# A gated mix of linear attention and a mixture of experts: sums by head as fp32 products in four column strips, reciprocals spread through scratch memory

## The chip, the cores and the metric

The kernel runs on one core of a Trainium2 chip. TensorE (PE) multiplies matrices: it holds a weight tile of up to 128 x 128 (loaded by a row named PEld) and streams up to 512 columns through it, into PSUM. VectorE (DVE), ScalarE (ACT) and GpSimd (POOL) work on up to 128 partitions by some hundred elements. DMA transfers are issued by the sequencer of SyncE (SP), of GpSimd or of ScalarE, each in its own order. The metric is the device time of one execution in microseconds (us), lower is better.

## The reference

Sequence 2048, width 512, 32 heads of 16, 8 experts of 1792 hidden units, all experts used for each token (K = E = 8), everything in fp32:

```python
phi = lambda t: jnp.where(t > 0, t + 1, jnp.exp(t)) + 1e-6
pq, pk = phi(q), phi(k)
kv = jnp.einsum("bhsd,bhse->bhde", pk, v)
z = jnp.einsum("bhsd->bhd", pk)
num = jnp.einsum("bhqd,bhde->bhqe", pq, kv)
den = jnp.einsum("bhqd,bhd->bhq", pq, z)[..., None] + 1e-6
o = num / den
...
a = o @ wo
b = sum over e of softmax(x @ w_gate)[e] * (silu(x @ w1[e]) @ w2[e])
g = sigmoid((x * gate_w).sum(-1, keepdims=True))
out = g * a + (1 - g) * b
```

(The last lines are condensed.) The change concerns `den`: for each query and head a sum over the head's 16 features of phi(q) times z, its reciprocal times the gate g, and the product of that with phi(q).

## The kernel before, in words

**Number format.** Most products run in a reduced fp32 type (F32R). To keep precision, each operand is split into a high part (a rounded copy) and a low part (the remainder), and `mm3` (lines 57 to 60) issues three products: high by high, high by low, low by high. Its lines 58, 59 and 60 in the profile are most of TensorE's work. Plain fp32 products exist in few places: the state (L885), the folding of the output weights (`fold`, L895, four products with 512 moving columns) and the normaliser (L904).

**Stages.** `keys` projects the keys and collects sums over the sequence. `experts` then runs one long loop over ticks `u`. In a tick, `up` issues the products of the first expert layer (group `g = u // 7`, step `k = u % 7`) and `tick(n)`, with `n = u - 58`, those of the second layer, each time as one level of a seven-product block scheme. A tick is filled with six products of each, twelve in all; `other()` is the work of VectorE, ScalarE and the queues beside them, issued ahead of the tick's second-layer products, and `mid()` issues these and what is to follow them. The order is written out by hand; each engine works through its own instructions in that order. The attention output is treated as one more expert (parts `A`), whose "hidden" values are phi(q) times the reciprocals.

**Queries.** phi(q) is computed early and put into DRAM scratch (`pqd`, one 128 x 512 tile for each of 2 x 2 blocks of 512 queries and 4 chunks of features). Beside four of the expert parts (`m.beside`) the loop works on one block `i` of 512 queries each. `s` counts the ticks from the part's start:

- `s = -3`, `queries_load` (L953 on): on SP's queue the sums z (`zcd`, high and low parts, 2 x 32 columns for each chunk) and a spreading matrix of zeros and ones (`spd`) come into one raw tile `Q.az`, and the four chunks of phi(q) into another.
- `s = 0..3`, `queries_first`: ScalarE makes the high part of phi(q) + EPS (L63, tile `az`), VectorE the low part (L86). `queries_last` (L996): TensorE multiplies both by `Q.z[:, s]`, 64 weight columns (32 heads by the high z, 32 by the low z), into one bank `dn` with the tag "a", accumulating over the four chunks.
- `s = 4`: ScalarE copies the low half out of PSUM, VectorE adds the high half (L976): `Q.r`, 32 heads x 512 queries.
- `s = 5..8`: VectorE takes reciprocals, 128 columns a tick (L980). `s = 9`: it multiplies by the gate (L982). `s = 10`: high part by ScalarE, remainder by VectorE (L985), into rows of `Q.un`.
- `s = 14..17`: TensorE multiplies the spreading matrix with these (L1000), so that each of the 128 features of a chunk has its head's reciprocal, in a PSUM bank with the tag "a".
- `s = 15..18`: VectorE multiplies phi(q) + EPS by it (L988), and SP stores the chunk back to `pqd`.

Accumulations into `acct` (L815) go by GpSimd's queue, two or so at the end of a part's phases; between `s = 5` and `s = 18` of a block there is none. `normaliser` (L901 to L911) computes z once, early in the loop. Tiles with the tag "a" share two PSUM banks; "rm" (raw tiles) has two buffers, "ot" (`out_tile`) four.

Of the kernel before, what the change touches and what calls it, by code (L numbers as in the profile page):

```python
# [37 lines left out]
def f32(ap):  # L38
    return ap.bitcast(F32)


@with_exitstack
def gated_mix_kernel(ctx: ExitStack, tc: tile.TileContext, xT, x, wk, wv, wqkv_q, wo, wm, out):
    nc = tc.nc
    PS = bass.MemoryType.PSUM

    const = ctx.enter_context(tc.tile_pool(name="const", bufs=1))
    xpool = ctx.enter_context(tc.tile_pool(name="xpool", bufs=14))
    w1p = ctx.enter_context(tc.tile_pool(name="w1p", bufs=1))
    psum = ctx.enter_context(tc.tile_pool(name="psum", bufs=1, space=PS))  # L50
    dram = ctx.enter_context(tc.tile_pool(name="dram", bufs=1, space=bass.MemoryType.DRAM))
    ctx.enter_context(tc.manual_schedule())

    m = SimpleNamespace(nc=nc, tc=tc, const=const, xpool=xpool, w1p=w1p, psum=psum, v=nc.vector,
                        xT=xT, x=x, wk=wk, wv=wv, wq=wqkv_q, wo=wo, wm=wm, out=out)

    def mm3(ps, wh, wlo, xh, xl, start, stop):
        nc.tensor.matmul(ps, wh, xh, start=start, stop=False, skip_group_check=True)  # L58
        nc.tensor.matmul(ps, wh, xl, start=False, stop=False, skip_group_check=True)  # L59
        nc.tensor.matmul(ps, wlo, xh, start=False, stop=stop, skip_group_check=True)  # L60

    def act_copy(dst, src, scale=1.0, bias=0.0):
        nc.scalar.activation(dst, src, AF.Copy, scale=scale, bias=bias)  # L63

    def ps_tile(name, tag, bufs=None):
        return psum.tile([P, TB], F32, name=name, tag=tag, bufs=bufs or {"a": 2, "b": 1, "c": 1, "dn": 4}[tag])

    m.mm3, m.act_copy, m.ps_tile = mm3, act_copy, ps_tile


    def phi_first(dst, src):
        nc.scalar.activation(dst, src, AF.Exp)
        nc.scalar.activation(src, src, AF.Relu)

    def phi_last(dst, src):
        nc.vector.scalar_tensor_tensor(dst, dst, 1.0, src, op0=ALU.min, op1=ALU.add)

    def phi(dst, src):
        phi_first(dst, src)
        phi_last(dst, src)  # L80

    def eps_high(h, d):
        act_copy(h, d, bias=EPS)

    def eps_low(lo, d, h):
        nc.vector.scalar_tensor_tensor(lo, d, EPS, f32(h), op0=ALU.add, op1=ALU.subtract)  # L86

    m.phi, m.phi_first, m.phi_last, m.eps_high, m.eps_low = phi, phi_first, phi_last, eps_high, eps_low
    m.ident = const.tile([P, P], F32, name="ident")


    def x_tile(name, tag="x"):
        return xpool.tile([P, 2, TB], F32R, name=name, tag=tag, bufs=14 if tag == "x" else 2)

    m.x_tile = x_tile
    m.XO = [[None] * 7, [None] * 7]
    m.xstash = dram.tile([7, 2, P, 2 * TB], F32, name="xstash")
    m.w2stash = [dram.tile([P, 2, D], F32, name=f"w2stash{i}") for i in range(7 * (E * NPAIR + 2) // 2)]
    m.wgtd = dram.tile([E + 1, S], F32, name="wgtd")
    m.acct = dram.tile([2, 2, KT, P, TB], F32, name="acct")  # L100
    m.pqd = dram.tile([2, 2, KT, P, TB], F32, name="pqd")
    m.wpd = [dram.tile([P, D], F32, name=f"wpd{c}") for c in range(KT)]
    m.zcd = dram.tile([P, KT * 2 * NH], F32, name="zcd")
    m.spd = dram.tile([P, KT * P], F32, name="spd")

    X = [[SimpleNamespace(e=e, h=h, n=NPAIR) for e in range(E)] for h in range(2)]
    A = m.A = [SimpleNamespace(e=E, h=h, n=2) for h in range(2)]
    M = E // 2  # L110

    m.parts = [*X[0], *X[1][:M], A[0], *X[1][M:], A[1]]
    at = 0
    for part in m.parts:
        part.t0, at = at, at + 7 * part.n
    m.NTICK = at
    m.groups = [(part, q) for part in (A[0], *X[0], *X[1][:M], A[1], *X[1][M:]) for q in range(part.n)]
    m.NG = len(m.groups)
    for part in m.parts:
        part.gs = [g for g, (p, _) in enumerate(m.groups) if p is part]  # L120
    m.G1 = X[1][0].gs[0]

    m.beside = [*X[1][:2], *X[1][M:M + 2]]

    misc = ExitStack()
    m.misc = misc.enter_context(tc.tile_pool(name="misc", bufs=1, side="right"))


    def pad(pool):
        nc.gpsimd.memset(pool.tile([P, 24], F32, name="pad", tag="pad", bufs=1), 0.0)  # L130

    m.pad = pad
    weights(m)
    keys(m)
    experts(m, misc)


# [181 lines left out]
def keys(m):  # L319
# [113 lines left out]
    def bands(t):  # L433
        if t == 5:
            band(mask.rearrange("p (b e) -> p b e", e=DH), [[-DH, P // DH], [0, DH]], 1)
        elif t == 6:
            band(maskh, [[P, KT], [-DH, NH]], 1)
        elif t == 7:

            spread = m.w1p.tile([P, 2, D], F32, name="spread", tag="ws", bufs=2)[:, 0]  # L440
            nc.gpsimd.memset(spread[2 * NH:], 0.0)
            for i in range(2):
                band(spread[i * NH:(i + 1) * NH].rearrange("p (c f) -> p c f", c=KT), [[P, KT], [1, P]], -DH)
            nc.gpsimd.dma_start(m.spd, spread)

    pk = {}

# [130 lines left out]
def experts(m, misc):  # L578
# [322 lines left out]
    def normaliser():  # L901
        ps = ps_tile("z", "dn")[:, :KT * NH]
        for c in range(KT):
            nc.tensor.matmul(ps[:, c * NH:(c + 1) * NH], m.pks[:, c * P:(c + 1) * P], m.ones, start=(c == 0),  # L904
                             stop=True, skip_group_check=True)
        zf = r_tile("zf")[:, :KT * NH].rearrange("p (c f) -> p c f", c=KT)
        zc = r_tile("zc", F32R)[:, :2 * KT * NH].rearrange("p (c j f) -> p c j f", c=KT, j=2)
        v.scalar_tensor_tensor(zf, ps.rearrange("p (c f) -> p c f", c=KT), S * EPS, m.maskh, op0=ALU.add, op1=ALU.mult)
        v.tensor_copy(zc[:, :, 0], zf)
        v.tensor_sub(zc[:, :, 1], zf, f32(zc[:, :, 0]))  # L910
        nc.sync.dma_start(m.zcd, f32(zc).rearrange("p c j f -> p (c j f)"))  # L911

    def gates(step):
        g = m.lg[:, :, :E]
# [33 lines left out]

    Q = SimpleNamespace()

    def queries_load(i):  # L953
        if i % 2 == 0:
            Q.az = m.raw_tile(f"az{i}", F32R)
            Q.z = Q.az[:, :2 * KT * NH].rearrange("p (c f) -> p c f", c=KT)
            Q.spread = Q.az[:, 2 * KT * NH:2 * KT * NH + D].rearrange("p (c f) -> p c f", c=KT)
            Q.un = Q.az[:, 2 * KT * NH + D:2 * KT * NH + 3 * D].rearrange("p (j t) -> p j t", j=2)
            nc.sync.dma_start(f32(Q.az[:, :2 * KT * NH]), m.zcd)
            nc.sync.dma_start(f32(Q.az[:, 2 * KT * NH:2 * KT * NH + D]), m.spd)  # L960
        Q.d = m.raw_tile(f"pq{i}").rearrange("p (c t) -> p c t", c=KT)
        for c in range(KT):
            nc.sync.dma_start(Q.d[:, c], m.pqd[i // 2, i % 2, c])

    def queries_first(i, s):
        h, j = divmod(i, 2)
        if 0 <= s < KT:
            m.eps_high(Q.un[:, 0], Q.d[:, s])
            m.eps_low(Q.un[:, 1], Q.d[:, s], Q.un[:, 0])
        elif s == 4:  # L970
            r = Q.r = out_tile(f"r{i}")[:NH]
            Q.gate = out_tile(f"rg{i}")[:NH]
            at = (2 * h + j) * TB
            nc.sync.dma_start(Q.gate, m.wgtd[E:E + 1, at:at + TB].to_broadcast([NH, TB]))
            act_copy(r, Q.ps[NH:2 * NH], bias=EPS)
            v.tensor_add(r, Q.ps[:NH], r)  # L976
            nc.gpsimd.memset(f32(Q.un[2 * NH:, 0]), 0.0)
        if 5 <= s < 9:
            r = Q.r[:, (s - 5) * P:(s - 4) * P]
            v.reciprocal(r, r)  # L980
        elif s == 9:
            v.tensor_mul(Q.r, Q.r, Q.gate)  # L982
        elif s == 10:
            act_copy(Q.un[:NH, 0], Q.r)
            v.tensor_sub(Q.un[NH:2 * NH, 0], Q.r, f32(Q.un[:NH, 0]))  # L985
        if 15 <= s < 15 + KT:
            d = Q.d[:, s - 15]
            v.scalar_tensor_tensor(d, d, EPS, Q.ps, op0=ALU.add, op1=ALU.mult)  # L988
            nc.sync.dma_start(m.pqd[h, j, s - 15], d)

    def queries_last(i, s):
        if 0 <= s < KT:
            if s == 0:
                Q.ps = ps_tile(f"dn{i}", "a")
            for j in range(2):
                nc.tensor.matmul(Q.ps[:2 * NH, :], Q.z[:, s], Q.un[:, j], start=(s == 0 and j == 0),  # L996
                                 stop=(s == KT - 1 and j == 1))
        elif 14 <= s < 14 + KT:
            Q.ps = ps_tile(f"n{i}_{s}", "a")
            nc.tensor.matmul(Q.ps, Q.spread[:, s - 14], Q.un[:, 0], start=True, stop=True)  # L1000


    def load_query(part, i):
# [227 lines left out]
```

## Time and profile before

| | |
|---|---|
| three runs | 2349.44, 2350.26 (median), 2350.53 us |
| the profiled execution | 2350.77 us, its span 2349.1 us |
| mean granted TensorE clock | 0.999 |
| VectorE, share of the span | 77% |
| ScalarE, share of the span | 60% |
| GpSimd, share of the span | 7% |

Rows of the profile read: line, engine, operation, tile written <- tiles read, shape, count; then busy time in us and the mean duration in ns. In the view by tile, a row has the shortest, median and longest duration in ns and the first and last start. In the timeline, a row has its start and its duration in us. A TensorE row begins when the product is issued and its end is modelled, so rows of following products overlap.

### The profile page before, as it was taken

How to read it: one execution, taken by the hardware profiler on the slowest of the kernel's cores; microseconds unless marked ns; L12 is line 12 of the kernel's file. 1: busy time of each engine (PE TensorE's matmuls, PEld its weight loads, DVE VectorE, ACT ScalarE, POOL GpSimd, SP SyncE). 2: the span in 40 equal slices, each digit the busy share in tenths (PEclk: the TensorE clock that was granted, in tenths of full speed). 3: DMA queues.
4: the chain of work that ended last, by engine and by line, in shares of the span. 5: the costliest groups of instructions: out<-in, count | busy, mean ns of one | idle time of the engine just before them, and what ended most of it. 6: DMA issues, size and time to landing. Idle time of an engine off the chain costs nothing.

```text
span 2349.1 us, 31301 instructions
## 1 busy us (share of the span) xinstructions
PE 2338.4 (100%) x10492; PEld 1935.4 (82%) x10492; DVE 1811.9 (77%) x3102; ACT 1419.3 (60%) x2655; POOL 158.7 (7%) x222
## 2 busy tenths in 40 slices
PE   9999999999999999999999999999999999999999
PEld 8877888888888888888888888888888888888887
DVE  6798888888888888888677768776676777766666
ACT  6686666666666656666555555555565655555553
POOL 2101000000000000000000000000011000000101
PEclk9999999999999999999999999999999999999999
DMA  7898888988889898988845455654556655555566
GB/s 225 239 311 249 264 288 249 278 263 267 268 267 275 256 290 252 271 269 262 287 144 170 152 172 153 182 186 144 163 166 188 182 150 174 162 166 166 165 220 207
DMA packets 299345, 513.23 MB, mean 218 GB/s; under 512 B 24352, under 2 KB 193840, under 8 KB 298800
## 3 DMA queue, kind: packets, MB, share of 16 engines
q1 hardware_dynamic: 274992, 464.10, 59.8%
q0 software_dynamic: 23344, 46.49, 10.8%
q8 instruction: 82, 1.34, 0.2%
q10 hardware_dynamic: 848, 0.66, 0.1%
q14 instruction: 79, 0.65, 0.1%
HBM read 343.43 MB, written 163.52 MB: 216 GB/s over the span
## 4 chain that ended last, share of the span: by engine, by line
PE 97%; DVE 1%; DMA 1%; issue 0%; ACT 0%; POOL 0%; DVEq 0%; ACTq 0%; POOLq 0%
PE p L58 16%; PE p L60 16%; PE p L59 16%; PE a L58 8%; PE a L60 8%; PE a L59 8%; PE c L59 4%; PE c L58 4%; PE c L60 4%; PE b L60 2%; PE b L59 2%; PE b L58 2%; PE g L451 2%; DMA w2stash<-w 1%; PE y L58 1%; PE y L60 1%
## 5 line engine op out<-in xcount | busy, mean ns | idle before, releaser
L58 PE MATMUL p<-ho,w 128*128 128x512 f32 x1620 | 631.4, 390 | 0.8 <-DVE d L844 0.6
L60 PE MATMUL p<-ho,w 128*128 128x512 f32 x1620 | 630.3, 389 | 0.0
L59 PE MATMUL p<-ho,w 128*128 128x512 f32 x1620 | 630.3, 389 | 0.0
L760 DVE TENSOR_TENSOR ho<-s,ho 128x512 fp32r<-128x512 f32 x784 | 537.2, 686 | 71.2 <-ACT ho L63 67.6
L63 ACT ACTIVATE ho<-s 128x512 fp32r<-128x512 f32 x784 | 487.3, 623 | 21.0 <-PE p L60 8.5
L58 PEld LDWEIGHTS p<-ho,w 128*128 128x128 f32 x1620 | 304.0, 188 | 66.7 <-ACT p L63 1.8
L60 PEld LDWEIGHTS p<-ho,w 128*128 128x128 f32 x1620 | 304.2, 188 | 63.2
L59 PEld LDWEIGHTS p<-ho,w 128*128 128x128 f32 x1620 | 304.1, 188 | 63.0
L63 ACT ACTIVATE o<-rs 128x512 fp32r<-128x512 f32 x224 | 129.1, 576 | 172.7 <-PE a L60 111.7
L690 DVE TENSOR_TENSOR s<-c,s 128x512 f32<-128x512 f32 x116 | 80.2, 692 | 188.6 <-PE c L60 178.7
L63 ACT ACTIVATE o<-rm 128x512 fp32r<-128x512 f32 x240 | 137.5, 573 | 99.8 <-PE a L60 77.4
L63 ACT ACTIVATE s<-a 128x512 f32<-128x512 f32 x116 | 69.5, 599 | 146.9 <-PE a L60 140.3
L63 ACT ACTIVATE ws<-rm 128x512 fp32r<-128x512 f32 x203 | 114.7, 573 | 66.2 <-DMA w2stash<-ws 59.3
L619 ACT ACTIVATE s<-s 128x512 f32<-128x512 f32 x224 | 138.7, 619 | 9.9 <-DVE s L696 6.6
L619 ACT ACTIVATE s<-b 128x512 f32<-128x512 f32 x112 | 67.2, 600 | 112.4 <-PE b L60 100.3
L205 DVE TENSOR_TENSOR o<-rm,o 128x512 fp32r<-128x512 f32 x180 | 122.9, 683 | 0.1
L205 DVE TENSOR_TENSOR o<-rs,o 128x512 fp32r<-128x512 f32 x168 | 114.5, 681 | 0.6 <-ACT o L63 0.6
L219 DVE TENSOR_TENSOR ws<-rm,ws 128x512 fp32r<-128x512 f32 x154 | 105.5, 685 | 0.5 <-ACT ws L63 0.5
L696 DVE TENSOR_TENSOR s<-a,s 128x512 f32<-128x512 f32 x116 | 80.0, 689 | 32.8 <-PE a L60 32.5
L63 ACT ACTIVATE b<-a 128x512 f32<-128x512 f32 x116 | 67.1, 579 | 58.1 <-PE a L60 58.0
L63 ACT ACTIVATE s<-c 128x512 f32<-128x512 f32 x116 | 69.0, 595 | 25.6 <-PE c L60 25.6
L815 POOL DMA_DIRECT2D acct<-c x30 | 25.6, 854 | 794.8 <-DVE c L809 779.8
(321 smaller groups left out, 4540.5 us busy)
## 6 DMA issues: line engine op xcount, KB each, us to landing
w<-w2stash SPq DMA_DIRECT2D x403, 512.0 KB, 4.0
w2stash<-ws SPq DMA_DIRECT2D x357, 256.0 KB, 4.2
rm<-wm SPq DMA_DIRECT2D x228, 256.0 KB, 5.2
rs<-wm SPq DMA_DIRECT2D x108, 256.0 KB, 4.0
wb<-wgtd SPq DMA_DIRECT2D x16, 512.0 KB, 5.2
acct<-c POOLq DMA_DIRECT2D x30, 256.0 KB, 5.6
acct<-d POOLq DMA_DIRECT2D x30, 256.0 KB, 5.5
acct<-k POOLq DMA_DIRECT2D x30, 256.0 KB, 5.5
```

Of the source, the lines that this page charges most:

```text
L58: nc.tensor.matmul(ps, wh, xh, start=start, stop=False, skip_group_check=True)
L59: nc.tensor.matmul(ps, wh, xl, start=False, stop=False, skip_group_check=True)
L60: nc.tensor.matmul(ps, wlo, xh, start=False, stop=stop, skip_group_check=True)
L63: nc.scalar.activation(dst, src, AF.Copy, scale=scale, bias=bias)
L205: v.tensor_sub(two(o, 1), src, f32(two(o, 0)))
L219: v.tensor_sub(two(w, 1), src, f32(two(w, 0)))
L451: nc.tensor.matmul(ps, xk((0, 0, 1)[j], tb, k, tt * P, (tt + 1) * P), gw[g][:, (0, 1, 0)[j], k, :], start=(k == 0 and j == 0), stop=(k == ...
L619: nc.scalar.activation(dst, src, AF.Silu)
L690: v.tensor_add(sn[g, 2], bank[g, "c"], sn[g, 2])
L696: v.tensor_add(sn[g, 3], bank[g, "a"], sn[g, 3])
L760: v.tensor_sub(h[1], s, f32(h[0]))
L815: nc.gpsimd.dma_start(m.acct[part.h, j, dt], s, accum_op=ALU.add)
```

## The change

The sums by head are taken with plain fp32 products, without splitting. z is kept as one fp32 matrix, 32 columns a chunk. Chunk c's product goes to partitions 32c to 32c + 31 of one bank, so the four products have four different column strips of the array and do not accumulate onto each other: z is masked by head (`maskh`), so of the 32 heads in each strip only the chunk's own eight have a sum. All four are issued in tick 3. EPS is added to phi(q) in place by ScalarE. The copy out of PSUM, the reciprocals and the gate's product run on all 128 partitions. The spreading matrix and its products are gone: the eight rows of each strip that hold sums are written to a DRAM scratch `rd`, and read back with each row repeated for 16 partitions, into three buffers beside z (the fourth chunk uses the first buffer again, after tick 15's product). These transfers are on GpSimd's queue.

```diff
-    m.zcd = dram.tile([P, KT * 2 * NH], F32, name="zcd")
-    m.spd = dram.tile([P, KT * P], F32, name="spd")
+    m.zcd = dram.tile([P, KT * NH], F32, name="zcd")
+    m.rd = dram.tile([2, 2, NH, TB], F32, name="rd")
...
-        elif t == 7:
-            spread = m.w1p.tile([P, 2, D], F32, name="spread", tag="ws", bufs=2)[:, 0]
-            nc.gpsimd.memset(spread[2 * NH:], 0.0)
-            for i in range(2):
-                band(spread[i * NH:(i + 1) * NH].rearrange("p (c f) -> p c f", c=KT), [[P, KT], [1, P]], -DH)
-            nc.gpsimd.dma_start(m.spd, spread)
...
-        zc = r_tile("zc", F32R)[:, :2 * KT * NH].rearrange("p (c j f) -> p c j f", c=KT, j=2)
         v.scalar_tensor_tensor(zf, ps.rearrange("p (c f) -> p c f", c=KT), S * EPS, m.maskh, op0=ALU.add, op1=ALU.mult)
-        v.tensor_copy(zc[:, :, 0], zf)
-        v.tensor_sub(zc[:, :, 1], zf, f32(zc[:, :, 0]))
-        nc.sync.dma_start(m.zcd, f32(zc).rearrange("p c j f -> p (c j f)"))
+        nc.sync.dma_start(m.zcd, zf.rearrange("p c f -> p (c f)"))
...
     def queries_load(i):
         if i % 2 == 0:
-            Q.az = m.raw_tile(f"az{i}", F32R)
-            Q.z = Q.az[:, :2 * KT * NH].rearrange("p (c f) -> p c f", c=KT)
-            Q.spread = Q.az[:, 2 * KT * NH:2 * KT * NH + D].rearrange("p (c f) -> p c f", c=KT)
-            Q.un = Q.az[:, 2 * KT * NH + D:2 * KT * NH + 3 * D].rearrange("p (j t) -> p j t", j=2)
-            nc.sync.dma_start(f32(Q.az[:, :2 * KT * NH]), m.zcd)
-            nc.sync.dma_start(f32(Q.az[:, 2 * KT * NH:2 * KT * NH + D]), m.spd)
+            az = m.raw_tile(f"az{i}")
+            Q.z = az[:, :KT * NH].rearrange("p (c f) -> p c f", c=KT)
+            Q.by = [az[:, KT * NH + c * TB:KT * NH + (c + 1) * TB] for c in (0, 1, 2, 0)]
+            nc.sync.dma_start(az[:, :KT * NH], m.zcd)
...
     def queries_first(i, s):
         h, j = divmod(i, 2)
+
+        def spread(c):
+            heads = m.rd[h, j, c * P // DH:(c + 1) * P // DH]
+            nc.gpsimd.dma_start(Q.by[c], heads[:, None, :].to_broadcast([P // DH, DH, TB]))
+
         if 0 <= s < KT:
-            m.eps_high(Q.un[:, 0], Q.d[:, s])
-            m.eps_low(Q.un[:, 1], Q.d[:, s], Q.un[:, 0])
+            act_copy(Q.d[:, s], Q.d[:, s], bias=EPS)
         elif s == 4:
-            r = Q.r = out_tile(f"r{i}")[:NH]
-            Q.gate = out_tile(f"rg{i}")[:NH]
+            r = Q.r = out_tile(f"r{i}")
+            Q.gate = out_tile(f"rg{i}")
             at = (2 * h + j) * TB
-            nc.sync.dma_start(Q.gate, m.wgtd[E:E + 1, at:at + TB].to_broadcast([NH, TB]))
-            act_copy(r, Q.ps[NH:2 * NH], bias=EPS)
-            v.tensor_add(r, Q.ps[:NH], r)
-            nc.gpsimd.memset(f32(Q.un[2 * NH:, 0]), 0.0)
+            nc.sync.dma_start(Q.gate, m.wgtd[E:E + 1, at:at + TB].to_broadcast([P, TB]))
+            act_copy(r, Q.ps, bias=EPS)
...
         elif s == 9:
             v.tensor_mul(Q.r, Q.r, Q.gate)
+            for c in range(KT):
+                n = P // DH
+                at = c * (NH + n)
+                nc.gpsimd.dma_start(m.rd[h, j, c * n:(c + 1) * n], Q.r[at:at + n])
         elif s == 10:
-            act_copy(Q.un[:NH, 0], Q.r)
-            v.tensor_sub(Q.un[NH:2 * NH, 0], Q.r, f32(Q.un[:NH, 0]))
+            for c in range(KT - 1):
+                spread(c)
         if 15 <= s < 15 + KT:
             d = Q.d[:, s - 15]
-            v.scalar_tensor_tensor(d, d, EPS, Q.ps, op0=ALU.add, op1=ALU.mult)
+            v.tensor_mul(d, d, Q.by[s - 15])
             nc.sync.dma_start(m.pqd[h, j, s - 15], d)
+            if s == 15:
+                spread(KT - 1)

     def queries_last(i, s):
-        if 0 <= s < KT:
-            if s == 0:
-                Q.ps = ps_tile(f"dn{i}", "a")
-            for j in range(2):
-                nc.tensor.matmul(Q.ps[:2 * NH, :], Q.z[:, s], Q.un[:, j], start=(s == 0 and j == 0),
-                                 stop=(s == KT - 1 and j == 1))
-        elif 14 <= s < 14 + KT:
-            Q.ps = ps_tile(f"n{i}_{s}", "a")
-            nc.tensor.matmul(Q.ps, Q.spread[:, s - 14], Q.un[:, 0], start=True, stop=True)
+        if s == KT - 1:
+            Q.ps = ps_tile(f"dn{i}", "a")
+            for c in range(KT):
+                nc.tensor.matmul(Q.ps[c * NH:(c + 1) * NH, :], Q.z[:, c], Q.d[:, c], start=True, stop=True)
```

In the changed kernel the four products stand on line 993.

## The prediction, made before the changed kernel was run

> **What bounds the kernel now.** I read the page's first part (busy time), then its fourth (the chain of waits), then the list of waits of TensorE alone, then one stretch of the window view around the first changed block.
>
> ```profile
> PE 2338.4 (100%) x10492; PEld 1935.4 (82%) x10492; DVE 1811.9 (77%) x3102; ACT 1419.3 (60%) x2655; POOL 158.7 (7%) x222
> ...
> PE 97%; DVE 1%; DMA 1%; issue 0%; ACT 0%; POOL 0%; DVEq 0%; ACTq 0%; POOLq 0%
> ```
> ```profile
> PE a L58 <- DVE s L696: 3.9, 2, 3.2
> PE idle L515 <- POOL ones L423: 1.4, 1, 1.4
> PE p L58 <- DVE d L844: 0.6, 1, 0.6
> ```
> ```profile
> core 0: us, PE busy (x) PEld busy (x) DVE busy (x) ACT busy (x) POOL busy (x), PEclk, DMA share, GB/s
> 1240.00:1330.00 90.00, 90.00 (x398) 74.03 (x397) 67.73 (x118) 51.62 (x94) 3.06 (x4) 1.00 0.57 173
> ```
>
> TensorE is the bound: 97% of the chain is its own work, and it waits 5.9 us in all (3.9 + 1.4 + 0.6). In the 90 us that hold the first query block it is busy for all 90, at full clock, while VectorE works 67.7 and ScalarE 51.6. So TensorE time that a block no longer needs comes off the end one for one, and work taken from VectorE or ScalarE there is worth nothing by itself. There are four such blocks (512 queries each); they do not meet.
>
> **What is removed from TensorE.** A busy row is longer than the step between two products, because they overlap; only steps between starts can be added up. Before, a block has four pairs at L996 (ticks 0 to 3) and four single products at L1000 (ticks 14 to 17).
>
> ```profile
> 1260.39 0.63 PE L996 MATMUL dn<-az 128*64 128x512 f32 x2
> ...
> 1263.60 0.63 PE L996 MATMUL dn<-az 128*64 128x512 f32 x2
> ...
> 1274.58 0.39 PE L58 MATMUL p<-ho,w 128*128 128x512 f32 x1
> ...
> 1277.30 0.39 PE L58 MATMUL p<-ho,w 128*128 128x512 f32 x1
> ```
> ```profile
> 1300.42 0.39 PE L1000 MATMUL n<-az 128*128 128x512 f32 x1
> ...
> 1303.37 0.39 PE L1000 MATMUL n<-az 128*128 128x512 f32 x1
> ```
> ```profile
> L996 PE MATMUL dn<-az 128*64 128x512 f32 x32 | 10.2, 396 | 0.0
> L1000 PE MATMUL n<-az 128*128 128x512 f32 x16 | 6.2, 389 | 0.0
> ```
>
> A tick of twelve ordinary products lasts 1277.30 - 1274.58 = 2.72 us, 0.227 each. A tick with a pair lasts 1263.60 - 1260.39 = 3.21, so a pair costs 0.49; a tick with one spreading product lasts 1303.37 - 1300.42 = 2.95, so that costs 0.23. Per block 4 x 0.49 + 4 x 0.23 = 2.88 us go; the counts x32 and x16 say that this happens in all four blocks: 11.5 us.
>
> **What is added to TensorE.** Four products per block, all behind tick 3, with 32 weight columns and 512 moving columns, all fp32 instead of the reduced fp32 type. Their nearest rows are the four folds of the output weights, which are plain fp32 with 512 moving columns but 128 weight columns.
>
> ```profile
> L895 PEld LDWEIGHTS wp<-wo,kvt x8: 186/188/189, 110.8 to 118.5; 128*128 128x128 f32 x8
> L895 PE MATMUL wp<-wo,kvt x8: 591/592/697, 110.8 to 118.9; 128*128 128x512 f32 x8
> ```
> ```profile
> 114.00 1.02 PE L895 MATMUL wp<-wo,kvt 128*128 128x512 f32 x2
> 114.45 0.79 PE L58 MATMUL c<-t1h,o 128*128 128x512 f32 x1
> ...
> 116.00 0.39 PE L60 MATMUL c<-t1h,o 128*128 128x512 f32 x1
> 116.24 1.02 PE L895 MATMUL wp<-wo,kvt 128*128 128x512 f32 x2
> ```
>
> Four folds give eight records, so an fp32 product is two records, each with a weight load. From fold to fold are 2.24 us, of which six ordinary products (114.45 to 116.00) take 6 x 0.227 = 1.36; the fp32 product takes 0.88, a record 0.44. The block's new group is eight records. Nothing in this trace shares the array by columns, so its length is bounded from both sides:
> - nothing shared: 8 x 0.44 = 3.52 us;
> - all four side by side: 2 x 0.44 = 0.88 us.
>
> I take a value between, from the order. All TensorE rows start in program order, and the two records of a product need the same 32 columns: the second cannot start before the first has streamed. The first record of the next product then starts beside the second of this one, but not earlier. Eight records in order make five steps (first; second and next first, three times; last): 5 x 0.44 = 2.20 us. For changing to this narrower form and back I add 0.10. Its lower bound is 0.04, what a pair with 64 columns costs over two ordinary products (0.49 - 0.45); its upper bound is twice the part of an ordinary record that its successor normally covers, 2 x (0.39 - 0.23) = 0.32. So the group costs 2.30 where 2.88 went: -0.58 per block, **-2.3 us** in all.
>
> A rule of the Trainium skill, TensorEngine Tiling (Array Packing), Key Properties, speaks against the change: a change of the tiling mode drains TensorE. The 64-column pairs show at most 0.04 us that could be such a drain. If it were two full tails of 0.16 us, the upper bound above, the sum would be -1.4 us.
>
> **VectorE and ScalarE.**
>
> ```profile
> L63 ACT ACTIVATE r<-dn x4: 590/590/590, 1270.7 to 1983.9; 32x512 f32<-32x512 f32 x4
> L976 DVE TENSOR_TENSOR r<-dn,r x4: 679/679/679, 1271.3 to 1984.5; 32x512 f32<-32x512 f32 x4
> ```
> ```profile
> L63 ACT ACTIVATE az<-pq x16: 618/631/639, 1258.4 to 1980.5; 128x512 fp32r<-128x512 f32 x16
> L86 DVE SCALAR_TENSOR_TENSOR az<-pq,az x16: 683/692/693, 1259.4 to 1981.2; 128x512 fp32r<-128x512 f32 x16
> ...
> L63 ACT ACTIVATE az<-r x4: 615/615/615, 1287.2 to 2000.5; 32x512 fp32r<-32x512 f32 x4
> L985 DVE TENSOR_TENSOR az<-r,az x4: 680/681/682, 1287.9 to 2001.1; 32x512 fp32r<-32x512 f32 x4
> ```
>
> Per block VectorE loses four subtractions (0.69 each), the addition of two halves (0.68) and the remainder of the reciprocals (0.68), 4.1 us; ScalarE loses one copy (0.62). ScalarE's four additions of EPS stay, now in place. The reciprocals, the gate product and ScalarE's copy out run over 128 partitions instead of 32: other rows of 512 elements show 0.68 for 32 partitions and 0.69 for 128, so they cost the same. The last multiplications read SBUF instead of PSUM; the subtractions that go read SBUF too, at 0.69, so they keep their price. The two VectorE operations less at the normaliser, the GpSimd work less at start and SP's one small load instead of two lie beside a full TensorE. All of this counts as 0, since TensorE covers it; VectorE and ScalarE only get slack. TensorE's new wait is for ScalarE's fourth in-place addition in tick 3, where it used to wait for VectorE behind that, so it can only be earlier. The group reads out through the same PSUM bank, taken three ticks later and freed in the same tick 4, before the next user in tick 5.
>
> **The transfers.** The reciprocals now leave by four small writes on GpSimd's queue in tick 9, come back by three spreading reads (ticks 15 to 17 use them) and a fourth read into the first one's buffer, issued when tick 15's product is done and needed in tick 18.
>
> ```profile
> 1284.82 0.67 DVE L982 TENSOR_TENSOR r<-r,rg 32x512 f32<-32x512 f32 x1
> ...
> 1301.38 0.68 DVE L988 SCALAR_TENSOR_TENSOR pq<-pq,n 128x512 f32<-128x512 f32 x1
> ...
> 1310.59 0.68 DVE L988 SCALAR_TENSOR_TENSOR pq<-pq,n 128x512 f32<-128x512 f32 x1
> ```
> ```profile
> L1012 POOL DMA_DIRECT2D q<-pqd x16: 538/768/885, 1724.7 to 2246.0; - x16
> ...
> DMA to landing us min/median/max: 3.6/5.0/7.0
> ```
>
> A load of 256 KB by GpSimd is issued in 0.77 us and lands in 5.0 (up to 7.0). The four writes take 4 x 0.77 = 3.1 to issue; the last lands at the latest some 7.0 behind that, and a read behind it in 7.0: 1285.5 + 3.1 + 7.0 + 0.8 + 7.0 = 1303.4 at the very worst, by medians 1285.5 + 3.1 + 5.0 + 0.8 + 5.0 = 1299.4, for the third, needed two ticks after the first, at 1306.8. The first, which waits for the first write only, comes by medians at 1285.5 + 0.8 + 5.0 + 0.8 + 5.0 = 1297.1 against 1301.4. The fourth has 1310.6 - 1302.1 = 8.5 us and takes 5.8, at worst 7.8. So they are hidden, by 4 and 3 us. Behind VectorE's wait for one stand the splits of hidden blocks, which TensorE needs some four ticks later, and additions from PSUM, needed after about one tick. GpSimd has nothing else to issue between ticks 9 and 18. Cost 0.
>
> **The sum.** The profiled execution took 2350.8 us (span 2349.1 and 1.7 around it): 2350.8 - 2.3 = 2348.5. It lies 0.5 above the median of the runs, so against the median: **2348.0 us**.
>
> **The rivals.**
> - *All four side by side.* The second record of a product does not hold back the next product: the group costs 0.88 + 0.10 = 0.98, -1.90 per block, -7.6 us: 2342.7. For it: the four outputs lie in four different strips of 32 partitions, and no group waits for another. Against it: rows start in order. The Trainium skill, TensorE: Matmul & The Clock Gate, Measured speedup vs the span model, has products in different column strips start some 4 ns apart; it measured 2.38 times for three. No run here shows it, and it does not speak of products in two records.
> - *Nothing is shared* (the change doesn't do what it says): 3.52 + 0.10 = 3.62, +0.74 per block, +3.0 us: 2353.3. For it: no row of this trace has two products really running beside each other; each has 0.227 of its own.
> - *The other side: the narrow records drain.* If weight loads into the same rows but other columns cannot be hidden, each record takes its whole 0.592 us instead of 0.44: 8 x 0.592 + 0.10 = 4.84, +1.96 per block, +7.8 us: 2358.1. It makes the kernel slower from 0.35 us per record on ((2.88 - 0.10) / 8), by 0.2% from 0.49. For it: with 128 columns each record has a load of 188 ns to hide. Against it: 1935.4 us of loads lie beside a TensorE that is busy throughout.
> - *The fourth read is late.* If it needs more than 8.5 us, VectorE stands in tick 18; what goes beyond some 3 us more reaches TensorE. At 13 us it would be 1.5 us a block, +6 - 2.3: 2354.0. Against it: no landing above 7.0 among the rows quoted.
>
> **How the numbers follow.** Forecast 0.34; all side by side 0.33; nothing shared 0.10; drained 0.16; late read 0.07. TensorE's one long wait (3.2 us for VectorE at L696) lies far ahead of the blocks, in code that does not change; in a program with other addresses it may fall away or come twice, which I give 0.04 and 0.03, taken from the forecast and the middle cases. By 0.2% (4.7 us, about what a measurement here can tell from no change) faster is below 2345.6, slower above 2355.0: faster 0.33 + 0.04 = 0.37, slower 0.16 + 0.03 = 0.19, same the other 0.44. The range must take in the second case, with the smallest form change 2342.5, and reach towards the drained one, of which it leaves out about half: 2342 to 2357. The forecast's own range, by its form-change bounds, is 2347.7 to 2348.8.
>
> **What will show it.** On the line of the four products, the step from the first of the group to the next ordinary product: 2.3 us for the forecast, 1.0 all side by side, 3.6 nothing shared, 4.8 drained. Ticks 0 to 2 and 14 to 17 must shrink to 2.72. VectorE's last multiplications must have no idle time put down to a transfer, and TensorE's list of waits must stay as it is. A new TensorE wait for VectorE, or a group that is longer than 2.88, makes the forecast's sign wrong.

## The result, and the profile after

Eight runs of the changed kernel have a median of 2343.2 us (2342.29 to 2344.45), eight runs of the kernel before beside them 2350.3 us. The medians are 7.1 us apart. The ratio of the means is 0.9972, 95% interval 0.9964 to 0.9981: 6.7 us less (4.5 to 8.5). The time is inside the stated range, but it is that of the first rival (2342.7), not of the forecast (2348.0). The profiled execution has a span of 2341.4 us where the one before had 2349.1.

First the changed kernel's page, busy time and chain, then TensorE's list of waits:

```profile
PE 2331.0 (100%) x10476; PEld 1927.8 (82%) x10476; DVE 1794.9 (77%) x3076; ACT 1415.9 (60%) x2651; POOL 172.2 (7%) x242
...
PE 96%; DMA 1%; DVE 1%; ACT 0%; issue 0%; SPq 0%; POOL 0%; DVEq 0%; ACTq 0%; POOLq 0%
```
```profile
PE a L58 <- DVE s L689: 3.6, 2, 2.9
PE idle L508 <- POOL ones L423: 1.4, 1, 1.4
PE p L58 <- DVE d L837: 0.6, 1, 0.6
PE p L58 <- DMA w<-w2stash: 0.3, 1, 0.3
```

The bound is the same, and TensorE waits 5.9 us as before. The 7.7 us of span are TensorE's own work and its pace. The new group in the first block, in TensorE's timeline and in that of its weight loads (start, duration in us):

```profile
1267.71 0.39 PE L60 MATMUL p<-ho,w 128*128 128x512 f32 x1
1268.03 1.07 PE L993 MATMUL dn<-pq,az 128*32 128x512 f32 x8
1269.03 0.50 PE L58 MATMUL a<-n5h,o 128*128 128x512 f32 x1
1269.36 0.39 PE L59 MATMUL a<-n5l,o 128*128 128x512 f32 x1
```
```profile
1268.03 0.16 PEld L993 LDWEIGHTS dn<-pq,az 128*32 128x32 f32 x8 [0.35 <-issue]
1269.02 0.19 PEld L58 LDWEIGHTS a<-n5h,o 128*128 128x128 f32 x1 [0.84 <-issue]
```

Eight records take 1.00 us from the first to the next ordinary product, and all eight weight loads are done in 0.16 us. Asked for the first hundredths of a microsecond only (1267.9 to 1268.06), the timeline has four of the eight:

```profile
1268.03 0.64 PE L993 MATMUL dn<-pq,az 128*32 128x512 f32 x4
```

Up to 1268.4 it stays at these four. What still runs from 1268.68 on is the other four:

```profile
1268.48 0.61 PE L993 MATMUL dn<-pq,az 128*32 128x512 f32 x4
```

So four products start together, and their second records follow together 0.45 us later. Around the group the array loses a little: the step into it is 1268.03 - 1267.71 = 0.32 instead of 0.23, and the first step behind it 0.33. The whole tick:

```profile
1266.58 0.39 PE L58 MATMUL p<-ho,w 128*128 128x512 f32 x1
...
1270.52 0.39 PE L58 MATMUL p<-ho,w 128*128 128x512 f32 x1
```

3.94 us, less 2.72 for twelve ordinary products: a group costs 1.22 us. To compare kernels free of what happens elsewhere, I take the starts of the first second-layer product of tick -2, tick 5 and tick 21 of each block, subtract 2.72 us for each tick between them, and so get what a block's sums and its spreading cost TensorE (in the last row the second column holds waits and a slow stretch, told below):

| us of TensorE per block | sums by head | spreading |
|---|---|---|
| before | 1.94, 1.94, 2.15, 1.95 | 0.91 |
| changed | 1.22 each | 0.00 |
| one strip | 3.77 | 0.00 |
| two strips in turn | 2.11 | 0.00 |
| two strips, one after the other | 2.12 | 0.00 |
| one product a tick | 4.82 | 0.00 |
| sums changed only | 1.23 | 0.91 |
| one buffer for the spread | 1.22 | 8.1 to 9.5 |

Before, four blocks cost 7.98 + 3.64 = 11.6 us, after 4.9: 6.7 us are the change. Of the other 1.0 us of span, 0.6 lie at the very start, where the first products ran slowly for a while longer in the one execution than in the other (first row before, second after):

```profile
5.46 1.82 PE L451 MATMUL g<-g,x00h 128*128 128x256 f32 x8
```
```profile
5.44 1.19 PE L444 MATMUL g<-g,x00h 128*128 128x256 f32 x8
```

This code did not change. Another 0.2 is the long wait at L696, now L689 (3.15 to 2.94 us), in code that did not change either; in five of the variants below it is 2.3 to 2.8 us. So I take both as chance and not as the change.

### The profile page after: what moved, and what is told of

Same layout as the page of the kernel before. It is cut to its first block, busy times and chain, and to the rows that moved or that the text cites. A ratio compares the mean times of both kernels' runs of the same rounds, so it can differ in the third digit from the quotient of the medians.

```text
span 2341.4 us, 31241 instructions
## 1 busy us (share of the span) xinstructions
PE 2331.0 (100%) x10476; PEld 1927.8 (82%) x10476; DVE 1794.9 (77%) x3076; ACT 1415.9 (60%) x2651; POOL 172.2 (7%) x242
## 3 DMA queue, kind: packets, MB, share of 16 engines
q0 software_dynamic: 26080, 50.69, 11.6%
## 4 chain that ended last, share of the span: by engine, by line
PE 96%; DMA 1%; DVE 1%; ACT 0%; issue 0%; SPq 0%; POOL 0%; DVEq 0%; ACTq 0%; POOLq 0%
PE p L58 15%; PE p L59 15%; PE p L60 15%; PE a L58 9%; PE a L59 9%; PE a L60 9%; PE c L58 4%; PE c L59 4%; PE c L60 4%; PE b L60 2%; PE b L58 2%; PE b L59 2%; PE g L444 2%; PE y L58 1%; PE y L60 1%; PE y L59 1%
## 5 line engine op out<-in xcount | busy, mean ns | idle before, releaser
L689 DVE TENSOR_TENSOR s<-a,s 128x512 f32<-128x512 f32 x116 | 80.0, 689 | 41.4 <-PE a L60 41.4
```

The costliest lines, as they stand in the source:

```text
L689: v.tensor_add(sn[g, 3], bank[g, "a"], sn[g, 3])
```

## The experiments

Six variants of the changed kernel. The first three differ in the strips that the group's products go to (condensed):

```diff
             for c in range(KT):
-                nc.tensor.matmul(Q.ps[c * NH:(c + 1) * NH, :], Q.z[:, c], Q.d[:, c], start=True, stop=True)
+                nc.tensor.matmul(Q.ps[b * NH:(b + 1) * NH, :], Q.z[:, c], Q.d[:, c], start=first, stop=last)
```

with b the strip and first, last true for the first and last product of a strip; as z is masked by head, products of one strip may be added up. Rows of heads, copy and writes follow the strips.

**One strip** (b = 0).

> All four fp32 products go to the same 32 columns (partitions 0 to 31 of the bank) and accumulate; 32 instead of 128 partitions are copied out and inverted. Theory (products share the array only because they lie in different column strips): nothing can be shared, eight records of 0.44 us follow each other, the step from the group's first record to the next ordinary product is about 3.5 us instead of 1.00, +2.5 us per block, +10 us in all against the changed kernel, about 2353. Rival (a product with 32 weight columns is cheap by itself, whatever its place): the step stays near 1.0 us and the time near 2343.

2353.4 us (2351.7 to 2354.7), ratio to before 1.0015 (1.0006 to 1.0025). Products, then weight loads:

```profile
1268.27 3.62 PE L994 MATMUL dn<-pq,az 128*32 128x512 f32 x8
1271.82 0.50 PE L58 MATMUL a<-n5h,o 128*128 128x512 f32 x1
```
```profile
1268.27 0.14 PEld L994 LDWEIGHTS dn<-pq,az 128*32 128x32 f32 x2 [0.35 <-issue]
1268.72 0.11 PEld L994 LDWEIGHTS dn<-pq,az 128*32 128x32 f32 x1 [0.32 <-issue]
```

The same eight records now take 3.55 us, 0.43 apart: the rival is out. A narrow product is not cheap; the strips are what makes four of them cost 1.00. In one strip the products are also added up in the same rows of the bank, and no variant separates that from sharing columns; but ordinary products are added up in one bank too (lines 58 to 60) and start 0.23 apart. The loads show the limit in these runs: one ahead per strip, the next only when the record before has started.

**Two strips in turn** (b = c % 2) and **two strips, one after the other** (b = c // 2).

> Two strips, taken in turn by the products: strips 0, 1, 0, 1; products of one strip accumulate. Theory A (a record waits only for records of its own strip that stand ahead of it, the strips run freely): four records each, 4 x 0.44 = 1.76 us for the step, +3 us in all against the changed kernel, about 2346. Theory B (records start in program order, both records of a product one behind the other): starts 0, 1, 1, 2, 2, 3, 3, 4 steps, end after 5 x 0.44 = 2.2 us, about 2348. Theory C (in order, but the program holds the first records of all products ahead of the second ones): 0,1,0,1,0,1,0,1 runs in pairs, 1.76 us.

> Two strips, products in the order 0, 0, 1, 1. Theory A (a record waits only for its own strip, and the queue looks past waiting records without limit): 4 x 0.44 = 1.76 us, as with strips in turn. Theory B (program order, both records of a product together): strip 1 begins with the last record of strip 0: 3 x 0.44 + 4 x 0.44 = 3.1 us, about 2351.5. Theory C (program order, first records of all ahead of the second ones: 0,0,1,1,0,0,1,1): starts 0, 1, 1, 2, 2, 3, 3, 4 steps, 2.2 us, about 2348.

2347.0 us (2344.7 to 2347.4) and 2346.8 us (2344.5 to 2348.4), ratios 0.9986 (0.9977 to 0.9996) and 0.9988 (0.9979 to 0.9997). In turn, then one after the other, with the loads of the latter:

```profile
1267.90 1.91 PE L994 MATMUL dn<-pq,az 128*32 128x512 f32 x8
1269.74 0.50 PE L58 MATMUL a<-n5h,o 128*128 128x512 f32 x1
```
```profile
1267.18 1.92 PE L994 MATMUL dn<-pq,az 128*32 128x512 f32 x8
1269.03 0.51 PE L58 MATMUL a<-n5h,o 128*128 128x512 f32 x1
```
```profile
1267.18 0.15 PEld L994 LDWEIGHTS dn<-pq,az 128*32 128x32 f32 x4 [0.35 <-issue]
1267.64 0.12 PEld L994 LDWEIGHTS dn<-pq,az 128*32 128x32 f32 x2 [0.30 <-issue]
1268.07 0.12 PEld L994 LDWEIGHTS dn<-pq,az 128*32 128x32 f32 x2 [0.30 <-issue]
```

They take 1.84 and 1.85 us, four records deep. The second is the telling one: with the four records of strip 0 ahead of those of strip 1, program order would have taken 3.1 us (or 2.2, if the first records of all products stood ahead). The run times alone would not tell 2.2 from 1.85 (2348 against runs of 2344.5 to 2348.4); the step does. Asked for 1267.1 to 1267.5 only, the timeline of one after the other has two of the eight records, that of one strip, for as long from its start, only one (first row one after the other, second row one strip, 1268.2 to 1268.6):

```profile
1267.18 0.63 PE L994 MATMUL dn<-pq,az 128*32 128x512 f32 x2
```
```profile
1268.27 0.62 PE L994 MATMUL dn<-pq,az 128*32 128x512 f32 x1
```

So strip 1 starts with strip 0, and four loads at once and then two by two say the same. Of the three theories only A fits: a record waits for its own strip and not for what stands ahead of it in another. Where the records are put into this order, in the engine's queue or already when an fp32 product is taken apart into records, no row tells.

**One product a tick** (each of ticks 0 to 3 issues its own chunk's product, in its own strip).

```diff
-        if s == KT - 1:
-            Q.ps = ps_tile(f"dn{i}", "a")
-            for c in range(KT):
+        if 0 <= s < KT:
+            if s == 0:
+                Q.ps = ps_tile(f"dn{i}", "a")
+            for c in (s,):
```

> The four products keep their four strips but are issued one in each of ticks 0 to 3, with twelve ordinary products between them. Theory (the gain needs the four next to each other): a step of about 0.88 us four times plus the changes of form, 3.6 to 4.4 us per block instead of 1.22, +10 to +13 us in all, 2353 to 2356. Rival (narrow products run beside ordinary ones or are cheap by themselves): near 2343.

2356.8 us (2356.0 to 2358.2), ratio 1.0030 (1.0018 to 1.0042); above the upper end of what was expected.

```profile
1262.12 0.39 PE L60 MATMUL p<-ho,w 128*128 128x512 f32 x1
1262.44 1.04 PE L994 MATMUL dn<-pq,az 128*32 128x512 f32 x2
1263.41 0.50 PE L58 MATMUL a<-n3h,o 128*128 128x512 f32 x1
1263.75 0.39 PE L59 MATMUL a<-n3l,o 128*128 128x512 f32 x1
```

One product alone costs as much as four together: 0.97 us to the next, and 4.82 / 4 = 1.21 with the steps around it. Ordinary products do not run beside a narrow one here. The price of going to the narrow form and back stands in these rows too: a visit costs 1.21 or 1.22 where two record steps are 2 x 0.43 = 0.86, so 0.35, with one product or with four. The fp32 type alone is not what costs it: the fold, fp32 at full width between ordinary products, took no more than its two records (0.88). Whether 32 columns of the reduced type would cost it, no run shows.

**Sums changed only.** The sums stay as changed, the spreading is TensorE's again (128 rows of the spreading matrix, four single products, no transfers, no remainder).

```diff
+            act_copy(Q.un, Q.r)
...
-            v.tensor_mul(d, d, Q.by[s - 15])
+            v.tensor_mul(d, d, Q.ps)
...
+        elif 14 <= s < 14 + KT:
+            Q.ps = ps_tile(f"n{i}_{s}", "a")
+            nc.tensor.matmul(Q.ps, Q.spread[:, s - 14], Q.un, start=True, stop=True)
```

> Only the sums are changed: four fp32 products in four strips as in the changed kernel, but the reciprocals are spread by four single products per block as before, with a spreading matrix of 128 rows, and no transfers. It leaves out the low part of the reciprocals. Theory (each part of the change is worth its TensorE time, and the transfers cost nothing): four products of 0.23 us per block come back, 4 x 4 x 0.23 = 3.7 us more than the changed kernel, about 2347. Rival (the transfers of the changed kernel cost time that TensorE's row does not show, some 1 us a block): this kernel is no slower than the changed one, 2343 or less.

2347.8 us in the middle, but from 2345.2 to 2355.6; ratio 0.9995 (0.9985 to 1.0004), in itself unclear. The block is not: a tick with a spreading product lasts 2.95 us again,

```profile
1299.81 0.39 PE L58 MATMUL p<-ho,w 128*128 128x512 f32 x1
...
1302.76 0.39 PE L58 MATMUL p<-ho,w 128*128 128x512 f32 x1
```

and each of the four blocks is 0.91 us longer than in the changed kernel, 3.6 us in all, with the sums at the same price. So the two parts of the change add up, and the transfers take nothing back.

**One buffer for the spread.** Each chunk's read waits for the product of the chunk before.

```diff
-            Q.by = [az[:, KT * NH + c * TB:KT * NH + (c + 1) * TB] for c in (0, 1, 2, 0)]
+            Q.by = [az[:, KT * NH + c * TB:KT * NH + (c + 1) * TB] for c in (0, 0, 0, 0)]
...
-            for c in range(KT - 1):
-                spread(c)
+            spread(0)
...
-            if s == 15:
-                spread(KT - 1)
+            if s < 14 + KT:
+                spread(s - 14)
```

> The repeated reciprocals of all four chunks go through one buffer, so that each read is issued only when the product of the chunk before is done (the changed kernel does so for the fourth chunk only). Theory (the transfers are hidden only by their lead): a read takes 0.6 us to issue and 4.5 us to land, so the four products of VectorE follow each other at some 5.9 us instead of 2.7, the last is 9 us late; VectorE waits for transfers some 3 us three times a block, and what goes beyond some 3 us of cover reaches TensorE, 3 to 6 us a block, 2355 to 2367. Rival (VectorE has enough lead that lateness never reaches TensorE): 2343 to 2345, with the waits on VectorE only.

2376.7 us (2376.4 to 2379.0), ratio 1.0121 (1.0104 to 1.0137): worse than expected by 10 us. VectorE's waits between 1290 and 1320 us, its last product of the block, and TensorE behind it:

```profile
DVE pq L982 <- DMA az<-rd: 9.0, 3, 3.5
```
```profile
1314.74 0.69 DVE L982 TENSOR_TENSOR pq<-pq,az 128x512 f32<-128x512 f32 x1 [3.50 <-DMA az<-rd]
```
```profile
1310.16 0.39 PE L60 MATMUL p<-ho,w 128*128 128x512 f32 x1
1316.09 0.80 PE L58 MATMUL a<-n6h,o 128*128 128x512 f32 x1 [5.55 <-DVE s L689]
1316.69 0.63 PE L59 MATMUL a<-n6l,o 128*128 128x512 f32 x1
...
1321.38 0.63 PE L58 MATMUL c<-n1h,o 128*128 128x512 f32 x1
1321.81 0.47 PE L59 MATMUL c<-n1l,o 128*128 128x512 f32 x1
```

VectorE waits three times for some 3 us, as expected, and the addition at L689 behind its last product is what TensorE waits for, 5.55 us in this block and up to 7.1 in the others. What had been left out follows: from 1316.09 to 1321.81 the products start 0.43 us apart instead of 0.23, which costs another 5.72 - 13 x 0.227 = 2.8 us in this block. The granted clock is 0.50 from 1316.2 to 1321.2, after 1.00 from 1304 to 1310. The same pair, a wait and then a stretch of products at 0.43 us, stands at L696 in the kernel before (3.15 us) and at L689 in the changed one (2.94 us). With shorter waits at that place it comes and goes: it is there after 2.3 us (two strips in turn) and 2.5 (one strip), and not after 2.7 (sums changed only) and 2.8 (two strips, one after the other). The Trainium skill, TensorE: Matmul & The Clock Gate, Part 1, says that the array's clock is halved after an idle window of about 3.4 us until it has been busy for another; the trace agrees with the halved pace, but not with that length, as waits of 2.3 to 3.15 us were followed by it here.

## Why the prediction was right and wrong

- **TensorE is the bound, and what it no longer does comes off the end**: right. What a block's TensorE work lost, 6.7 us in four blocks, is in the span, and TensorE's waits stayed at 5.9 us.
- **2.88 us removed per block**: right. Measured 1.94 + 0.91 = 2.85, and 0.2 more in the third block, where the first pair had been late by that much.
- **A record of 0.44 us, two for a product**: right; 3.55 us for eight in one strip, and 0.43 from load to load.
- **"The second cannot start before the first has streamed. The first record of the next product then starts beside the second of this one, but not earlier"**: this is the step that failed. The first half is true (one strip). The second half is not: the next product's first record starts beside this one's first, since another strip does not wait. Two strips, one after the other, show it where the order of the program does not help. The five steps (2.20) are two (0.88); that is 1.3 us per block, over 5 us, more than the whole gap between forecast and result. The forecast's own range (2347.7 to 2348.8) is missed by 4.5 us; the stated one holds the result because it was stretched to take in the rival that proved right.
- **0.10 us for the change of form**: mis-sized; a visit to the narrow form costs 0.35 us, a little above the upper bound that had been worked out from the uncovered part of a record (0.32). The 64-column pairs, whose 0.04 was the lower bound, were no measure of it. In the rows, the narrow loads start only with the group's first product, with the load unit idle for 0.35 us before, and the ordinary load behind the group at 1269.02, 0.01 ahead of its product at 1269.03. The rule on draining in the Trainium skill, TensorEngine Tiling (Array Packing), Key Properties, fits this: the trace agrees for the form with 32 columns, with 0.35 us for the way there and back, while the pairs with 64 columns showed only 0.04.
- **All four side by side** (0.33) is what happened, for its reason, and its 0.98 us per block was 1.22, because of the form change. Its sum of -7.6 has about 0.25 us a block too much gain and leaves out the late pair, against 6.7 in the blocks; that it came so near the 7.1 between the medians is partly luck. The Trainium skill, TensorE: Matmul & The Clock Gate, Measured speedup vs the span model, has strips start together; the trace agrees: four starts by 0.03 us behind the first.
- **Nothing shared** and **the narrow records drain one by one**: both out. One strip is the former, at 3.77 us. The latter's 0.592 us for each record is nowhere: in one strip they follow each other by 0.43. That one product a tick comes to 4.82 us, near the 4.84 of this rival, is chance: it makes four visits to the narrow form.
- **VectorE, ScalarE and the normaliser at 0**: right; with 17 us less of VectorE's work nothing but TensorE's own time moved.
- **The transfers hidden**: right, and for the first three reads by more than thought. GpSimd's rows of the first block and VectorE's products:

```profile
1284.47 2.06 POOL L977 DMA_DIRECT2D rd<-r  x4 [25.36 <-DVE r L973]
1286.83 1.24 POOL L959 DMA_DIRECT2D az<-rd  x2 [0.29 <-issue]
1289.36 0.59 POOL L959 DMA_DIRECT2D az<-rd  x1 [1.29 <-DMA rd<-r]
1301.03 0.59 POOL L959 DMA_DIRECT2D az<-rd  x1 [11.08 <-DVE pq L983]
```
```profile
1300.04 0.69 DVE L983 TENSOR_TENSOR pq<-pq,az 128x512 f32<-128x512 f32 x1
...
1308.57 0.68 DVE L983 TENSOR_TENSOR pq<-pq,az 128x512 f32<-128x512 f32 x1
```

The first three reads are issued by 1290.0, ten microseconds before they are used (four writes take 2.06 us to issue, not 3.1); the fourth has 7.5 us from issue to use, and a read lands in 4.5 (median of 16; 3.6 to 7.6). VectorE has no wait for them in any block. That this cover is needed is what one buffer shows: the rival of the late read was priced without the slow stretch that follows a long wait.

## What to carry to other kernels

Where TensorE is the bound and a product needs only 32 weight columns, four of them in four column strips cost what one does, but only side by side: issue them together, since each visit to the narrow form costs 0.35 us here and a lone one costs as much as four. Before ruling a change like this in or out by the order of the instructions, ask which resource a queued instruction really waits for, and try both ends in the sum. A long wait on a busy TensorE can cost more than its length: here a slow stretch followed each one of 2.9 us or more, and two of those between 2.3 and 2.8.

## What the hardware showed that was not expected

Records of an fp32 product in one column strip do not hold back records of another strip, even when in the program all four records of the one stand ahead: eight records in one, two and four strips take 3.55, 1.84 and 1.00 us, that is 8, 4 and 2 steps of 0.43 and about 0.13. A single narrow fp32 product between ordinary ones costs 1.21 us, where the fold's full-width one cost 0.88: narrower weights are dearer, not cheaper.
